# Filler transposes of a delta-rule kernel: on a PSUM tile that nobody reads, or left out

## The chip, the cores and the metric

The kernel runs on one core of a Trainium2 chip. The metric is the device time of one execution in microseconds (us); the lower, the better. Engines: PE (TensorE), DVE (VectorE), ACT (ScalarE), POOL (GpSimd) and SP, which issues the DMAs.

## The reference

Three stages follow each other, in fp32. First a delta-rule recurrence over 768 positions for 4 batches of 8 heads, each with a 48 x 48 state:

```
k_n = k / (norm(k) + 1e-06)
for t in range(768):
    y[t]  = q[t] @ state
    v_old = state^T k_n[t]
    state = state + beta[t] * outer(k_n[t], v[t] - v_old)
```

Then a gated MLP with mixing over positions:

```
h = relu(x @ w_in)                      # 384 -> 1024
u, v = h[..., :512], h[..., 512:]
v_n = layer_norm(v)
v_s = w_spatial @ v_n + b_spatial       # over the 768 positions
x = (u * v_s) @ w_out                   # 512 -> 384
```

Then a rotation with a second mixing over positions:

```
theta = x @ w_theta
y = w_tok_r @ (x * cos(theta)) + w_tok_i @ (x * sin(theta))
u = x + y
out = u + relu(u @ w_ch)
```

## The kernel before

The recurrence is worked in 48 chunks of 64 positions, 12 for each batch, one after the other; all 8 heads of a batch go together. I call a chunk a step, numbered 0 to 47. Eight steps make a round, and for each round the inverse of 32 small triangular matrices is needed ahead of its first step. The large matrix products of the later stages (L1050; three fp32r products for each fp32 one) have no part in the recurrence, and those whose batch is through with it are set between its steps.

What a step does, with the lines of the profile:

- `chain`: L906 (PE, into PSUM `ru`), L910 (DVE subtracts, giving `rt`), L920 (PE, into `ru`), two copies of `ru` into the state tile `W` (ACT or DVE, L482 or L488), L936/L938 (PE, into PSUM `s`), two copies of `s` into the next `W`. Each needs the one before it. L948/L949 (PE, into `py`) give the output.
- `gram`, for a step eight to twelve later: L711/L716 (PE, into PSUM `gp`), read by DVE at L736 (`GX`) and L740 (`pp`). A mask from POOL (L671) goes in.
- `jit`: L845/L846 (PE, into PSUM `m`), rounds 0 and 1 only.
- `invert`, once for each round: some 60 dependent DVE instructions (L779, L791) and three transpositions (L757, L795, L800), then twice L818 (PE, into `gp`), ACT copies `gp` to `ct`, L824 (PE, into `gp`), ACT copies `gp` to `GX`. L920 of the round's first step needs the result.

`gp` is one PSUM tile of two banks, `GPt`, used by L705, L711, L716, L818 and L824. `ru` is another, `RUt`, of which L906 and L920 use columns 0 to 95 of each bank.

The order of the instructions on every engine is made by a list scheduler, `Plan.run`, at build time. It holds a model of durations and of the clock of PE, which is granted at one of two levels. Where its model has PE idle for a while ahead of a task, and the activity of PE is low, it puts `k` constant transposes of the identity matrix ahead of the task (`self.filler(k)`, L514). They compute nothing that is used; they keep the array busy. They write columns 0 to 127 of `GPt`. The scheduler doesn't model what `gp` is doing at that time, but the program waits for it: a write to `gp` follows the last reads of it, and a read of `gp` that comes later in the program follows that write. A large product is chosen in place of a small task (`pe_pick`) when the modelled activity of PE, fillers included, is low. In the first inversion there is a burst of fillers besides (`BURST0`, 60 of them).

Of the kernel before, what the change touches and what calls it, by code (L numbers as in the profile page):

```python
# [97 lines left out]
BANK = 180.0  # L98
# [34 lines left out]
class Half(Buf):  # L133
# [6 lines left out]
    t = property(lambda self: self.whole.t[:, self.i], lambda self, x: None)  # L140
# [10 lines left out]
def P0_READY(plan, free):  # L151
    t = plan.ident
    return t.end is not None and t.end + t.extra + 1000.0 < free


class Plan:
# [76 lines left out]
    def pe_pick(self, l, s0, c):  # L233
# [27 lines left out]
            return best  # L261
        return c

    def run(self):
        self.warm, self.win, self.acc, self.burst = False, 0, 0.0, False
        self.hist = []
# [19 lines left out]
        free = dict.fromkeys(self.ENGS, 0.0)  # L286
        held = dict.fromkeys(self.ENGS, 0)
        lock = {"DVE": (0.0, 0.0), "POOL": (0.0, 0.0)}
        mode = 0
        lands, dmaq = [0.0] * LANES, 0.0  # L290
        cand = [t for t in self.tasks if t.left == 0]
        n = 0
        while cand:
            per = {}
            for t in cand:
# [9 lines left out]
                for e, dur in t.opts:  # L305
                    r = 0.0
                    for d in deps:
                        x = d.end + d.extra + (self.SAME[e] if d.eng == e else self.TAIL[d.eng] + self.LAT[e])
                        if x > r:
                            r = x  # L310
                    for b in t.banks:
                        o = b.last
                        if o is not None and o.eng != e and o.end + BANK > r:
                            r = o.end + BANK
# [9 lines left out]
                    k = s + dur + (0.0 if t.crit else BIAS[e])  # L324
# [16 lines left out]
            s, e, t, dur = pick  # L341
            t.eng, t.start, t.end = e, s, s + dur
            if e == "PE":
                gap = s - free[e]
                if s < FILL_END and self.warm and not t.big and P0_READY(self, free[e]):
                    need = 0
                    for win in (SLIDE, FILL_WIN):
                        h = s + dur - win
                        a = dur * t.act
                        for x0, x1, ac in reversed(self.hist):  # L350
                            if x1 <= h:
                                break
                            a += (x1 - max(x0, h)) * ac
                        need = max(need, int((FILL_LOW * win - a) // 78.0) + 1)
                    room = int((gap - FILL_EDGE) // 82.0)
                    more = max(need, int(FILL_ACT * gap // 82.0))
                    k = max(min(need, FILL_K), min(room, more))
                    if k > 0:
                        f0 = free[e] + (100.0 if mode else 0.0)
                        f1 = self.pe_run(PEFILL, f0, 82.0 * k)[0]  # L360
                        self.hist.append((f0, f1, PEFILL.act))
                        mode = 0
                        self.filler(k)
                        self.filled += k
                        s = max(s, f1)
                        t.start, t.end = s, s + dur
                if t.mode != mode:
                    t.start = s = s + (100.0 if mode else 140.0)
                mode = t.mode
                t.end = self.pe_run(t, s, dur)[0]  # L370
                self.hist.append((s, t.end, t.act))
                if t.big:
                    self.credit -= dur
# [26 lines left out]
class Bytes(float):  # L400
    n = 0
# [40 lines left out]
def kernel(  # L442
# [18 lines left out]
    nc = tc.nc  # L461
    mm = nc.tensor.matmul
    eng = {"ACT": nc.scalar, "DVE": nc.vector, "POOL": nc.gpsimd, "SP": nc.sync}
    P = Plan()
# [13 lines left out]
    def ring(pl, tag, shape, dtype=F32, bufs=1):  # L478
        return Ring(pools, pl, shape, dtype, tag, bufs)
# [28 lines left out]
        return [("SP", x)]  # L508


    def filler(n):

        for _ in range(n):
            nc.tensor.transpose(GPt[:, 0:128], ident.t, ident.t)  # L514

    P.filler = filler

# [17 lines left out]
    def single(pl, name, shape, dtype=F32):  # L535
        return Buf(tile_=pools[pl].tile(shape, dtype, name=name))

    ident = single("const", "ident", [128, 128])
# [10 lines left out]
    GPt = pools["ps_a"].tile([128, 1024], F32, name="gp")  # L549
    r_gp = Fixed(pools, "ps_a", GPt, "gp")  # L550
    RUt = pools["ps_a"].tile([128, 2, 512], F32, name="ru")
    r_ru = Fixed(pools, "ps_a", RUt[:, :, 0:2 * D], "ru")
    r_s = ring("ps_a", "s", [128, HP, D], F32, 1)
    PYt = pools["ps_a"].tile([128, HP, 128], F32, name="py")
    PY = Buf(tile_=PYt)
# [40 lines left out]
    def rnd(g):  # L596
        return divmod(g, RM)
# [590 lines left out]
    for g in range(NG):  # L1188
        r, j = rnd(g)
# [341 lines left out]
```

## Time and profile before

| | us |
|---|---|
| median of 3 runs | 807.89 (805.58 to 807.99) |
| the profiled execution | 812.74 |
| its span, first to last instruction | 811.0 |
| PE busy | 740.4 |
| DVE busy | 569.6 |
| ACT busy | 400.2 |
| L514 (filler), PE busy, 352 instructions | 63.3 |

The page gives the busy time of each engine, the chain of work that ended last, and groups of instructions by line. The trace behind it answers by line, by stage and in order of time. A busy PE is not PE at its peak: the rows of matmuls include the time that a result takes to come out, and at the lower clock they are longer. Idle time in front of an instruction is put down to what came last; a reader should look which engine then waited for which, and in which stage, since shares over the whole span mix stages with different limits.

### The profile page before, as it was taken

Reading aid. Unit: us, or ns where it says so; the run is one execution under the profiler, and the core shown is the slowest. Engines: PE = TensorE matmul, PEld = TensorE weight load, DVE = VectorE, ACT = ScalarE, POOL = GpSimd, SP = SyncE. Lnnn points to the kernel's source line nnn. Section 1 sums busy time; section 2 is a strip of 40 time slices with the busy share of each in tenths; the row PEclk is TensorE's granted clock in tenths of the full one; section 3 lists DMA queues with packets and bytes.
Section 4 is the critical chain, followed back from the end, with each engine's and each line's share of the span. In section 5 each row is a group of like instructions: output and inputs, shape, how many; then the busy total and the mean of one; then the engine's idle time right before and its main releaser. Section 6 shows DMA issues by size and latency. Waiting matters only on the chain.

```text
span 811.0 us, 22761 instructions
## 1 busy us (share of the span) xinstructions
PE 740.4 (91%) x9281; PEld 681.0 (84%) x9281; DVE 569.6 (70%) x1398; ACT 400.2 (49%) x878; POOL 154.4 (19%) x169
## 2 busy tenths in 40 slices
PE   4486889889887988998999999999999999999998
PEld 4385667768776776787898999999999999999997
DVE  5988797997991696994458745679565575556545
ACT  4837357657542455885567636155333342333321
POOL 2035344351421202141001100012111111111100
PEclk9999789989996699998999999999999999999999
DMA  7617567875776376776887720153020011002001
GB/s 217 205 44 205 153 178 196 242 207 153 208 217 195 108 213 204 217 220 178 244 261 244 220 90 1 65 161 109 25 84 27 27 37 53 25 26 83 1 1 59
DMA packets 93272, 109.56 MB, mean 135 GB/s; under 512 B 10096, under 2 KB 73968, under 8 KB 93168
## 3 DMA queue, kind: packets, MB, share of 16 engines
q1 hardware_dynamic: 93168, 108.11, 45.0%
q8 instruction: 73, 1.20, 0.6%
q14 instruction: 31, 0.25, 0.1%
HBM read 79.76 MB, written 26.61 MB: 131 GB/s over the span
## 4 chain that ended last, share of the span: by engine, by line
PE 64%; DVE 17%; DMA 6%; ACT 5%; issue 5%; SPq 2%; POOL 1%; POOLq 0%; DVEq 0%; ACTq 0%
PE m L1050 30%; PE y L1050 19%; PE gp L514 6%; DVE un L791 4%; DVE tmp L779 4%; DMA k<-in_vkn_dram 2%; DMA xr<-xd 2%; PE gp L824 1%; PE py L948 1%; DVE GX L736 1%; PE gp L818 1%; ACT ct L482 1%; PE s L936 1%; PE ru L920 1%; PE m L1357 1%
## 5 line engine op out<-in xcount | busy, mean ns | idle before, releaser
L1050 PE MATMUL m<-w,vh 128*128 128x256 f32 x576 | 112.1, 294 | 0.4 <-ACT uT L482 0.4
L1050 PEld LDWEIGHTS m<-w,vh 128*128 128x128 f32 x576 | 90.8, 194 | 3.3 <-ACT uT L482 0.6
L1050 PE MATMUL y<-wr,xTh 128*128 128x384 f32 x432 | 86.2, 337 | 0.0
L514 PE MATMUL gp<-ident 128*128 128x128 f32 x352 | 63.3, 327 | 24.3 <-DVE pp L740 8.1
L1050 PE MATMUL y<-w,xTl 128*128 128x384 f32 x432 | 83.9, 336 | 0.0
L1050 PE MATMUL m<-w,vl 128*128 128x256 f32 x288 | 82.1, 285 | 0.0
L1050 PEld LDWEIGHTS y<-wr,xTh 128*128 128x128 f32 x432 | 75.3, 188 | 0.0
L1050 PEld LDWEIGHTS y<-w,xTl 128*128 128x128 f32 x432 | 75.1, 188 | 0.0
L514 PEld LDWEIGHTS gp<-ident 128*128 128x128 f32 x352 | 47.9, 166 | 30.5 <-DVE pp L740 10.0
L791 DVE TENSOR_TENSOR un<-un,tmp 128x30 f32<-128x30 f32 (+21 forms) x209 | 71.0, 350 | 1.5
L779 DVE TENSOR_TENSOR tmp<-un 128x30 f32<-128x30 f32 (+21 forms) x209 | 67.6, 333 | 1.5
L1050 PEld LDWEIGHTS m<-w,vl 128*128 128x128 f32 x288 | 55.8, 194 | 0.0
L671 POOL TENSOR_TENSOR gm<-mask,ng 128x384 f32<-128x384 f32 (+1 forms) x52 | 43.2, 836 | 56.3 <-DVE pp L740 26.3
L1382 DVE TENSOR_SCALAR bgr<-m 128x384 int32<-128x384 f32 x22 | 12.2, 555 | 55.3 <-PE m L1050 55.3
L482 ACT ACTIVATE W<-ru 64x192 f32<-64x192 f32 x87 | 28.4, 326 | 45.9 <-PE ru L920 43.4
L1050 PE MATMUL m<-wo,gh 128*128 128x384 f32 x176 | 44.7, 334 | 0.0
L1050 PE MATMUL m<-xTh,wih 128*128 128x256 f32 x144 | 43.6, 303 | 0.9 <-ACT hv L482 0.9
L1050 PE MATMUL m<-xTl,wih 128*128 128x256 f32 x144 | 40.8, 283 | 0.0
L1050 PE MATMUL m<-xTh,wil 128*128 128x256 f32 x144 | 40.7, 283 | 0.0
L482 ACT ACTIVATE x<-m 128x384 f32<-128x384 f32 x13 | 6.4, 491 | 65.7 <-PE m L1050 65.7
L482 ACT ACTIVATE W<-s 48x192 f32<-48x192 f32 x78 | 25.6, 328 | 26.2 <-PE s L938 25.0
L1050 PE MATMUL m<-uh,wc 128*128 128x384 f32 x144 | 38.5, 337 | 0.0
(213 smaller groups left out, 1933.1 us busy)
## 6 DMA issues: line engine op xcount, KB each, us to landing
kq<-in_kqT_dram SPq DMA_DIRECT2D x96, 128.0 KB, 3.5
vk<-in_vkn_dram SPq DMA_DIRECT2D x48, 192.0 KB, 3.7
kg<-in_kgT_dram SPq DMA_DIRECT2D x32, 256.0 KB, 3.4
gd<-gt SPq DMA_DIRECT2D x24, 256.0 KB, 3.8
graw<-gd SPq DMA_DIRECT2D x24, 256.0 KB, 3.1
k<-in_vkn_dram SPq DMA_DIRECT2D x24, 192.0 KB, 4.0
xd<-xs SPq DMA_DIRECT2D x48, 96.0 KB, 3.0
xr<-xd SPq DMA_DIRECT2D x24, 192.0 KB, 3.2
```

The source lines that it names most:

```text
L482: nc.scalar.activation(out=out, in_=in_, func=func, **kw)
L514: nc.tensor.transpose(GPt[:, 0:128], ident.t, ident.t)
L671: eng[e].tensor_tensor(out=gm.t[:, lo:hi], in0=mask.t.unsqueeze(1).to_broadcast([128, hi - lo, CH]), in1=ng_b[r].t[:, j, 4 + lo:4 + hi].un ...
L736: A(o_dve(256), lambda e: nc.vector.tensor_tensor(out=gxj, in0=GX0()[:, :, 0] if fused else pv(), in1=gm.t[:, 2:6], op=ALU.mult), [ps, gm] ...
L779: eng[e].tensor_tensor(out=t3, in0=un.t[:, k:k + 1, 0:k].to_broadcast([128, m, k]), in1=un.t[:, t0:32:st, k:k + 1].to_broadcast([128, m, k ...
L791: eng[e].tensor_tensor(out=un.t[:, t0:32:st, 0:k], in0=un.t[:, t0:32:st, 0:k], in1=t3, op=ALU.add)
L818: mm(out=pv[q + 32:q + 64, u, :], lhsT=gx[q:q + 32, u0 + u, 32:64], rhs=un.t[q:q + 32, u0 + u, :], start=True, stop=True, tile_position=(q ...
L824: mm(out=pv[q:q + 32, u, :], lhsT=ct.t[q + 32:q + 64, u, :], rhs=gx[q + 32:q + 64, u0 + u, 32:64], start=True, stop=True, tile_position=(q ...
L920: mm(out=pu.t[o:o + 64, h, q * D:(q + 1) * D], lhsT=gx[i:i + 64, j * HP + slot(hp), :], rhs=rt.t[i:i + 64, hp, :], start=True, stop=True)
L936: mm(out=pss.t[0:48, hp, :], lhsT=kt[64:128, hp, :], rhs=w[64:128, 0, hp, :], start=f, stop=l, skip_group_check=True)
L1050: mm(out=view(), lhsT=a, rhs=c, start=(start and q == 0 and s_ == 0), stop=(stop and q == tot - 1 and s_ == 2))
L1382: P.add(o_dve(DM), lambda e: nc.vector.tensor_scalar(out=ni.t.bitcast(I32), in0=th(), scalar1=1.0 / TWO_PI, scalar2=None, op0=ALU.mult), [ ...
```

## The change

The filler gets an argument for where it writes. `P.spots` lists two buffers, `gp` and `ru`. Before the scheduler puts fillers ahead of a task, `spot` looks for the first of the two whose last issued user has, in the plan, been written and read to the end a margin (`BANK`, 180 ns) before the fillers would start. Fillers go there: to `GPt[:, 0:128]`, or to columns 128 to 255 of the first bank of `RUt`. If both are in use, there are no fillers at that place. The burst of the first inversion stays on `gp`.

```diff
+    def spot(self, f0):
+
+        for r in self.spots:
+            b = r.issued[-1] if r.issued else None
+            if b is None or all(t.end is not None and t.end + BANK <= f0 for t in (*b.writers, *b.readers)):
+                return r.tag
+        return None
...
-                    if k > 0:
-                        f0 = free[e] + (100.0 if mode else 0.0)
+                    f0 = free[e] + (100.0 if mode else 0.0)
+                    spot = self.spot(f0)
+                    if k > 0 and spot is not None:
                         f1 = self.pe_run(PEFILL, f0, 82.0 * k)[0]
                         self.hist.append((f0, f1, PEFILL.act))
                         mode = 0
-                        self.filler(k)
+                        self.filler(k, spot)
...
-    def filler(n):
-
+    def filler(n, spot="gp"):
+        out = GPt[:, 0:128] if spot == "gp" else RUt[:, 0, 128:256]
         for _ in range(n):
-            nc.tensor.transpose(GPt[:, 0:128], ident.t, ident.t)
+            nc.tensor.transpose(out, ident.t, ident.t)
...
+    P.spots = [r_gp, r_ru]
```

The scheduler's model sees other activity of PE afterwards, and so the whole order changes. Of 352 fillers 172 are left, 104 on `gp` (73 of them in one row at the start) and 68 on `ru`, in 20 rows of the order where there were 60. Lines behind the added method are 8 to 10 higher: L514 becomes L523, L818 L828, L824 L834, L920 L930, L1050 L1060.

Two places of PE's order show it. The first is the inversion of round 3, between steps 23 and 24. Before:

```order
L514 MATMUL gp<-ident 128x128 x5
L818 MATMUL gp<-un,GX_110 32x32 x32
L514 MATMUL gp<-ident 128x128 x13
L824 MATMUL gp<-GX_110,ct 32x32 x32
L514 MATMUL gp<-ident 128x128 x13
L818 MATMUL gp<-un,GX_110 32x32 x32
L514 MATMUL gp<-ident 128x128
L920 MATMUL ru<-rt,GX_110 64x48 x8
L514 MATMUL gp<-ident 128x128 x8
L824 MATMUL gp<-GX_110,ct 32x32 x32
```

And of the changed kernel, from the last pair of output matmuls of step 23 on:

```order
L959 MATMUL py<-kq,W_109 48x64
L523 MATMUL ru<-ident 128x128 x6
L834 MATMUL gp<-GX_110,ct 32x32 x32
L523 MATMUL ru<-ident 128x128 x13
L828 MATMUL gp<-un,GX_110 32x32 x32
L523 MATMUL ru<-ident 128x128
L930 MATMUL ru<-rt,GX_110 64x48 x8
L834 MATMUL gp<-GX_110,ct 32x32 x32
L523 MATMUL ru<-ident 128x128 x8
```

The fillers between the halves of the inversion write `ru` now; those ahead of the first half are gone, two and the output matmuls having moved behind it.

The second place is step 30, from its L906 on, ahead of the inversion of round 4. Before:

```order
L949 MATMUL py<-kq,W_109 48x64
L906 MATMUL ru<-W_108,kq 64x48 x8
L514 MATMUL gp<-ident 128x128 x3
L920 MATMUL ru<-rt,GX_110 64x48 x8
L514 MATMUL gp<-ident 128x128 x6
L936 MATMUL s<-W_108,vk 48x48
```

Of the changed kernel, the same step (`m` is the PSUM of the large products, `xTh`/`xTl` and `wih`/`wil` the two parts of x and of w_in):

```order
L916 MATMUL ru<-W_108,kq 64x48 x8
L1060 MATMUL m<-xTh,wih_140 128x256
L1060 MATMUL m<-xTl,wih_140 128x256
L1060 MATMUL m<-xTh,wil_143 128x256
L1060 MATMUL m<-xTh,wih_141 128x256
L1060 MATMUL m<-xTl,wih_141 128x256
L1060 MATMUL m<-xTh,wil_144 128x256
L930 MATMUL ru<-rt,GX_110 64x48 x8
```

Where fillers stood between L906 and L920, six large products of batch 1 stand now. Up to the last L920 the order has 126 products of 128x512 and 672 of 128x256, where there were 108 and 594. On DVE 382 rows stand ahead of the `rt` (L910) of step 8, where there were 333; ahead of that of step 23 it is 618 and 613.

## Rows read from the trace of the kernel before

**Rows 1.** The page: its line of the chain by line, and L514's group.

```profile
PE m L1050 30%; PE y L1050 19%; PE gp L514 6%; DVE un L791 4%; DVE tmp L779 4%; DMA k<-in_vkn_dram 2%; DMA xr<-xd 2%; PE gp L824 1%; PE py L948 1%; DVE GX L736 1%; PE gp L818 1%; ACT ct L482 1%; PE s L936 1%; PE ru L920 1%; PE m L1357 1%
...
L514 PE MATMUL gp<-ident 128*128 128x128 f32 x352 | 63.3, 327 | 24.3 <-DVE pp L740 8.1
```

**Rows 2.** By stage: stretch and length, engines' busy us, PE clock, DMA share, GB/s.

```profile
41.00:61.60 20.60, 18.56 (x329) 17.09 (x327) 16.52 (x48) 7.69 (x14) 7.52 (x8) 1.00 0.18 51
61.60:134.60 73.00, 58.98 (x1289) 48.66 (x1288) 61.15 (x165) 41.71 (x99) 31.11 (x38) 0.88 0.66 182
134.60:242.10 107.50, 95.85 (x2061) 81.33 (x2058) 98.71 (x268) 61.38 (x141) 38.98 (x44) 0.95 0.72 205
242.10:274.30 32.20, 26.46 (x441) 22.57 (x441) 9.62 (x24) 10.29 (x18) 4.76 (x5) 0.61 0.53 154
274.30:320.80 46.50, 40.65 (x824) 33.65 (x823) 38.55 (x89) 25.03 (x47) 11.10 (x10) 0.94 0.64 189
320.80:410.70 89.90, 87.48 (x1567) 73.90 (x1566) 62.53 (x170) 62.86 (x137) 13.83 (x14) 0.96 0.76 220
410.70:811.00 400.30, 395.11 (x2499) 387.60 (x2498) 250.23 (x503) 164.21 (x336) 41.75 (x37) 1.00 0.24 78
```

**Rows 3.** The same for L514 alone: PE, PE weight load, clock, DMA.

```profile
61.60:134.60 73.00, 20.82 (x105) 14.83 (x104) 0.88 0.66 182
134.60:242.10 107.50, 4.67 (x24) 2.76 (x24) 0.95 0.72 205
242.10:274.30 32.20, 14.79 (x65) 11.47 (x65) 0.61 0.53 154
274.30:320.80 46.50, 8.87 (x56) 5.88 (x55) 0.94 0.64 189
```

**Rows 4.** View of line L514, who waited for it: us, times.

```profile
  ACT ct L482: 9.4, 5
...
  DVE pp L740: 6.5, 5
```

**Rows 5.** Timeline of step 3: start us, us, engine, instruction [idle before, its releaser].

```profile
88.29 0.34 DVE L910 TENSOR_TENSOR rt<-ru,vk 128x192 f32<-128x192 f32 x1
...
88.42 3.15 PE L514 MATMUL gp<-ident 128*128 128x128 f32 x14 [1.71 <-DVE pp L740]
...
91.50 0.65 PE L920 MATMUL ru<-rt,GX 64*64 64x48 f32 x16
```

**Rows 6.** Timeline of the inversion of round 3, steps 23 and 24.

```profile
244.68 2.64 PE L514 MATMUL gp<-ident 128*128 128x128 f32 x15 [2.17 <-DVE GX L736]
...
247.35 0.43 DVE L740 TENSOR_TENSOR pp<-gp,gm 128x256 f32<-128x256 f32 x1 [2.23 <-PE gp L514]
...
249.30 1.20 PE L818 MATMUL gp<-un,GX 32*32 32x32 f32 x64
...
251.79 2.48 PE L514 MATMUL gp<-ident 128*128 128x128 f32 x13 [1.29 <-ACT ct L482]
...
254.21 1.92 PE L824 MATMUL gp<-GX,ct 32*32 32x32 f32 x64
...
257.41 3.04 PE L514 MATMUL gp<-ident 128*128 128x128 f32 x13 [1.29 <-ACT GX L482]
...
262.63 0.68 PE L920 MATMUL ru<-rt,GX 64*64 64x48 f32 x16
...
264.04 1.97 PE L514 MATMUL gp<-ident 128*128 128x128 f32 x8 [0.73 <-ACT ct L482]
```

**Rows 7.** Timeline behind step 47, large products, PE.

```profile
418.45 0.40 PE L1050 MATMUL m<-wih,xTh 128*128 128x512 f32 x1
418.69 0.40 PE L1050 MATMUL m<-wil,xTh 128*128 128x512 f32 x1
...
424.00 0.28 PE L1050 MATMUL m<-xTh,wih 128*128 128x256 f32 x1
424.12 0.28 PE L1050 MATMUL m<-xTl,wih 128*128 128x256 f32 x1
```

## The prediction

> **What bounds the kernel now.** I read the page first. TensorE (PE) is busy for most of the span; L514, the constant transposes of the filler, is 352 instructions in 63.3 us, with 24.3 us of idle time just before them, of which VectorE (DVE) reading `gp` ended the largest piece; and the chain that ended last lies on that line for 6% of the span, about 50 us [rows 1]. A filler computes nothing, so this is what the change touches. Then the table by stage, cut at the first L920 of steps 0, 8, 23, 25, 32 and 47 of the recurrence [rows 2]. It shows three regimes. From 410.7 us PE is busy for all but some 5 us of 400: the end is simply the recurrence's end plus the large products (L1050) still left. From 320.8 to 410.7 PE is at 97% (87.48 of 89.90 us). Before that PE has holes: subtracting busy time from length in the four rows from 61.6 to 320.8 leaves 14.0, 11.7, 5.7 and 5.9 us idle, 37 us, and the filler takes 20.82, 4.67, 14.79 and 8.87 us [rows 3]. So between 61.6 and 320.8 us PE spends about 86 us on nothing useful. DVE is the second bound there: 98.71 of 107.50 us in 134.6:242.1, 61.15 of 73 before it, but only 9.62 of 32.20 in 242.1:274.3, where everybody waits for everybody.
>
> Why the filler costs time is in the view of its line and in the timeline. It writes `gp`. Each of its instructions therefore waits until the last readers of `gp` are through, and the readers that come later wait for it: ACT `ct` 9.4 us, DVE `pp` 6.5 us [rows 4]. At 88.42 fourteen of them have waited 1.71 us for `pp` and run 3.15 us, while `rt`, which the next real step needs, is made by 88.63; L920 starts at 91.50 [rows 5]. In the inversion of round 3 it is worse: L818, ScalarE's copy, filler, L824, copy, filler, L818 follow each other with no overlap [rows 6].
>
> **The change part by part.** The compiled order has 172 fillers where there were 352: the 73 at the start stay, 68 others go to `ru`, 31 stay on `gp` at places where its last reader is planned to be done, 180 are gone. The scheduler plans anew with that, so the order of everything moves.
>
> *Start, 41 to 61.6 us.* Behind the burst of 73 stand 31 fillers in and around the first inversion. They now run beside the copies. The eight at 264.04 take 1.97 us at half clock [rows 6], so one is about 0.12 us at full clock; 31 of them and 2.04 us of idle PE [rows 2] are 5.8 us at most, and the copies themselves stay. I take 3.
>
> *Steps 0 to 8, 73.0 us.* 20.82 us of filling go almost entirely (104 to 11 instructions up to L920 of step 8). But the freed time isn't all gain: counting DVE's rows ahead of the `rt` of step 8, 382 stand there now and 333 before. Those 49, each by the duration of its twin in the trace, are some 16 us of DVE work pulled forward, of which about 5 ran before the end of the stage already. 61.15 + 11 = 72 us of DVE work don't fit in less than 73 to 76 us. I give this stage a loss of 3, which cancels the start.
>
> *Steps 8 to 23, 107.5 us.* What was pulled forward is missing here: ahead of the `rt` of step 23 only 5 DVE rows more stand than before, so the stage has some 9 us less on DVE (98.71 to 89.7). At the present 92 to 94% that is 96 us: 11 us gained. PE allows it: 95.85 less 4.67 of filler and 4.2 of products that moved ahead of the stage is 87 us.
>
> *Steps 23 to 25, 32.2 us.* Here the clearest gain lies [rows 6]. L818 starts at 249.30, behind 15 fillers (2.64 us) that waited for `GX` and for which `pp` then waits 2.23 us. Without them `pp` runs 2.2 us earlier and L818 can follow at about 245.7: 3.6 us. From L818 to L920 of step 24 the trace has 13.33 us. In the new order 8 fillers and a `py` group (taken as six fillers more) stand beside the first copy and 13 fillers beside the second, on `ru`, so that the longer of the two counts and not the sum: 1.2 + 1.65 + 1.2 + 1.55 + 1.2 = 6.8 us at full clock (L818's 1.20 at 249.30), about 10.6 at half clock (L824's 1.92 at 254.21). Gain 2.7 to 6.5. In step 24 the eight at 264.04 wait for `ct` ahead of L824; behind it and on `ru` they cost 0.3 to 1.8 us less, and the small fillers up to step 25 are gone, 1.5. Sum 8 to 13.4; as nobody waits for a filler any more, the clock should stand nearer to full, but the row of this stage says 0.61 now, so I take the middle, 10.5.
>
> *Steps 25 to 32, 46.5 us.* This stage takes up work. 18 products of 128x512 and 78 of 128x256 are ahead of the last L920 that weren't before (126 and 672, against 108 and 594), and here is where most join: with the filler gone the planner sees an idle array and gives it a product. PE was 40.65 us, less 8.87 filler, plus 13.5: 45.3 of 46.5 us. It will be the bound; I allow 3 us more length.
>
> *Steps 32 to 47.* 23 fillers now stand here (about 2.8 us), 1 us of products is gone, and PE has 2.4 us to spare: 0.
>
> *After step 47.* The 18 + 78 products no longer stand here. By starts that follow each other one is 0.24 us or 0.12 us [rows 7] (0.232 and 0.119 over longer runs), so 4.2 + 9.3 = 13.5 us, straight off the end, as PE is 99% busy. The first product that needs a new weight stands about as far behind step 47 as before, so nothing new should be late; I allow 1.5 us.
>
> Sum: -3 + 3 - 11 - 10.5 + 3 - 13.5 + 1.5 = -30.5 us. Against this stands what the rows can't price: PE without filler sits idle more often, and its clock may fall. It was granted 0.88 in steps 0 to 8 and 0.61 in 242.1:274.3 even with fillers [rows 2], since they stood waiting themselves. From below, no more cold time than now costs 0 (or gives a little back in 242.1:274.3); from above, if steps 0 to 8 run wholly at 1.2 GHz, the lower of the two levels, some 36 us of real PE work there become about 60, still under DVE's 72, and cost a few tenths per hand-over, some 5 us, and as much again in steps 8 to 23. Mostly hidden by DVE, it is nearer to the lower end; I take 4.5. That leaves **-26 us**. The profiled execution took 812.74 us for a span of 811.0, so its successor should be near 787; the median of the runs, 807.89, lies 4.85 lower, and I forecast **782 us**.
>
> The Trainium skill, page "TensorE: Matmul & The Clock Gate", part "The HAM clock gate", speaks against the change: the array's default state is the throttled one, and only activity releases it. By that rule 180 transposes fewer cost clock wherever nothing replaces them, which is the first rival; this trace bears it out only in part, as the stage with the lowest clock, 0.61, is also the one with the most filler per us.
>
> **The rivals.**
>
> *The clock decides, and it gets slower.* Place: steps 0 to 23, where almost no filler is left and products are few. The bare PE work there is about 36 + 84 = 120 us at 2.4 GHz, up to 85% longer at 1.2 (L824: 1.92 against 1.20; products double). The two stages last 180.5 us, and elsewhere the change still gives some 22 (inversion and products at their lower ends). With PE 95% full at most, 126 x (1 + 0.85c) = 202.5 gives c = 0.71: if PE is at the lower level for more than 71% of these stages the whole is slower; at 85% it would be 217 us there and 14 more than now in all: 822. For it: 0.88 and 0.95 are granted with fillers, some of which will have helped. Against: those are cold shares of 24 and 10%, and would have to become four times as large; the 0.95 was reached with 24 fillers in 107.5 us.
>
> *The moved products don't pay.* If steps 25 to 32 become wholly PE-bound and the recurrence waits for each product, the stage grows by what it took in, 13.5 instead of 3, and inputs of these products that land later than planned take 4 more: -11.5, 796. For it: PE would be 97% full. Against: 320.8 to 410.7 runs 97% full with just this mix.
>
> *The recurrence isn't bound by PE.* If steps 0 to 23 are held by DVE and loads alone and gain nothing, the inversion (10.5) and the products (13.5) less 8 of clock and stalls remain: -16, 792. For it: DVE at 92%, the DMA engines at 0.72 there.
>
> *The wait only moves to `ru`.* Eleven groups write `ru`, and L906 and L920 write it too; where ScalarE is later than planned, a filler waits for its copy and holds up PE as in rows 5, at 1.7 us each [rows 5]. If all do: 19 us of the gain gone, 801. Against: the groups of round 0 stand before the first use of `ru`, the others at least an L818 or L824 behind the last L920.
>
> *The change doesn't do what it says:* the scheduler's times are a plan, and where the chip is later, the fillers on `gp` still wait. But of 279 beyond the burst only 31 are left there, so for 808 the re-planned order would have to lose elsewhere all that is won, and I see no row for that.
>
> **How the numbers follow.** Forecast -26 with a spread of 8 either way: 0.55. Recurrence not bound by PE 0.13, products that don't pay 0.12, `ru` 0.08, nothing 0.03, clock 0.09, of which 0.01 ends within 0.3%. A measurement of this kernel can tell about 0.3% (2.4 us) from no change. Faster 0.55 + 0.13 + 0.12 + 0.08 = 0.88; same 0.04; slower 0.08. The range reaches from 765, where clock, stalls and the lengthening of steps 25 to 32 cost nothing (9), the inversion runs at full clock (3) and steps 8 to 23 are as full as DVE allows (5), to 801, the dearest of the smaller rivals; the clock case and the tails stay outside, under 2 in 10.
>
> **What would show it.** Right: the filler's line with under 15 us busy beyond the burst and hardly an idle time ended by DVE `pp`; L818 to L920 of step 24 in 7 to 10 us, not 13.3; step 23 near 231, step 25 near 253, step 47 near 397 us; then 388 us to the end. Wrong: a granted clock under 0.7 in steps 0 to 23; steps 25 to 32 over 53 us; PE waiting for a load or a copy in the 40 us behind step 47. The forecast falls if step 47 is reached at 405 or later, as then only the products are left.

## The result and the profile after

The changed kernel takes **786.50 us** (median; 785.66 to 791.06) where the kernel before took 807.94 beside it: a ratio of 0.9736, with a 95% interval of 0.9673 to 0.9799. Forecast were 782 us and a range of 765 to 801. The profiled execution of the changed kernel took 785.66 us, its span is 783.9 (before: 812.74 and 811.0).

The changed kernel by stage, cut as in [rows 2] at the first L930 (before: L920) of steps 0, 8, 23, 25, 32 and 47. The columns are the stretch and its length, the busy us of PE, PE's weight load, DVE, ACT and POOL, then PE's clock, the DMA share and GB/s:

```profile
41.00:59.80 18.80, 18.80 (x327) 17.54 (x326) 15.66 (x43) 6.83 (x11) 7.55 (x7) 1.00 0.20 56
59.80:136.70 76.90, 61.67 (x1283) 52.34 (x1286) 71.94 (x203) 50.42 (x121) 36.06 (x42) 0.68 0.68 195
136.70:237.90 101.20, 91.61 (x1983) 78.62 (x1975) 90.72 (x236) 50.67 (x112) 39.91 (x47) 0.91 0.72 205
237.90:253.10 15.20, 12.78 (x407) 10.83 (x406) 8.53 (x23) 9.50 (x18) 1.35 (x2) 1.00 0.84 252
253.10:304.80 51.70, 48.30 (x900) 40.70 (x900) 46.82 (x115) 34.07 (x73) 11.10 (x11) 0.97 0.71 214
304.80:398.10 93.30, 88.06 (x1533) 74.86 (x1528) 63.69 (x158) 61.15 (x125) 13.77 (x15) 0.96 0.75 224
398.10:783.90 385.80, 381.52 (x2403) 374.47 (x2402) 243.61 (x489) 157.07 (x323) 40.09 (x36) 1.00 0.23 74
```

Against [rows 2] the lengths changed by -1.8, +3.9, -6.3, -17.0, +5.2, +3.4 and -14.5 us; that is the whole of the 27.1 us between the spans. The execution before was 4.85 us above the median of its kernel's first three; by the medians the gain is 21.4 us. Two stages win clearly: the inversion of round 3 (32.2 to 15.2 us, and the clock there from 0.61 to 1.00) and the end behind step 47. Step 47 itself is reached only 12.6 us earlier (398.10 against 410.70).

The same stages for the filler alone, L523 (columns: PE, weight load, clock, DMA share, GB/s):

```profile
41.00:59.80 18.80, 14.54 (x102) 13.17 (x100) 1.00 0.20 56
59.80:136.70 76.90, 2.33 (x12) 1.63 (x11) 0.68 0.68 195
136.70:237.90 101.20, 1.02 (x4) 0.49 (x4) 0.91 0.72 205
237.90:253.10 15.20, 4.37 (x30) 3.23 (x30) 1.00 0.84 252
253.10:304.80 51.70, 0.00 (x0) 0.00 (x0) 0.97 0.71 214
304.80:398.10 93.30, 3.61 (x23) 2.47 (x23) 0.96 0.75 224
```

Behind the start the filler is 11.3 us where [rows 3] has 49.2. In the view of its line the two lists that follow, who made it wait and who waited for it, are empty; before, the first summed to 52.1 us, and the second, of which [rows 4] has two lines, to 26.2:

```profile
L523 PE MATMUL gp<-ident x104: 272/273/473, 40.2 to 340.7; 128*128 128x128 f32 x104
...
L523 PE MATMUL ru<-ident x68: 272/273/421, 52.2 to 249.8; 128*128 128x128 f32 x68
its engine sat idle before it (us, times) until:
who waited for it (us, times):
```

The inversion of round 3 in the changed kernel's timeline, which answers to [rows 6]:

```profile
238.50 1.20 PE L828 MATMUL gp<-un,GX 32*32 32x32 f32 x64 [0.19 <-DVE pp L750]
...
240.59 0.87 PE L523 MATMUL ru<-ident 128*128 128x128 f32 x6
241.39 1.07 PE L834 MATMUL gp<-GX,ct 32*32 32x32 f32 x56
...
243.21 1.64 PE L523 MATMUL ru<-ident 128*128 128x128 f32 x13
244.78 1.20 PE L828 MATMUL gp<-un,GX 32*32 32x32 f32 x64
...
246.17 0.45 PE L930 MATMUL ru<-rt,GX 64*64 64x48 f32 x16
```

From L828 to L930 are 7.67 us; the same way took 13.33 us in [rows 6]. The 13 fillers take 1.64 us, at full clock, and start while ScalarE copies `gp` to `GX`; before they took 3.04 us and started behind that copy, after 1.29 us of idle time.

### The profile page after: what moved, and what is told of

Same layout as the page of the kernel before. It is cut to its first block, busy times and chain, and to the rows that moved or that the text cites. A ratio compares the mean times of both kernels' runs of the same rounds, so it can differ in the third digit from the quotient of the medians.

```text
span 783.9 us, 22417 instructions
## 1 busy us (share of the span) xinstructions
PE 720.9 (92%) x9101; PEld 666.4 (85%) x9101; DVE 574.0 (73%) x1402; ACT 397.3 (51%) x871; POOL 155.2 (20%) x172
## 4 chain that ended last, share of the span: by engine, by line
PE 64%; DVE 17%; DMA 6%; ACT 6%; issue 4%; SPq 3%; POOL 1%; POOLq 0%; DVEq 0%; ACTq 0%
PE m L1060 32%; PE y L1060 20%; DVE tmp L789 4%; DVE un L801 3%; DMA bgr<-in_w_r_dram 2%; DMA vk<-in_vkn_dram 2%; PE gp L523 2%; ACT bgr L491 1%; SPq L528 1%; PE py L958 1%; PE gp L834 1%; PE ru L930 1%; PE m L1367 1%; PE gp L828 1%; PE ru L916 1%
## 5 line engine op out<-in xcount | busy, mean ns | idle before, releaser
L1060 PE MATMUL m<-w,vh 128*128 128x256 f32 x576 | 112.0, 294 | 0.7 <-DVE gt L1176 0.7
L1060 PEld LDWEIGHTS m<-w,vh 128*128 128x128 f32 x576 | 90.5, 193 | 3.6 <-DVE gt L1176 0.8
L1060 PE MATMUL y<-wr,xTh 128*128 128x384 f32 x432 | 86.2, 337 | 0.0
L1060 PE MATMUL y<-w,xTl 128*128 128x384 f32 x432 | 83.9, 336 | 0.0
L1060 PE MATMUL m<-w,vl 128*128 128x256 f32 x288 | 82.0, 285 | 0.0
L1060 PEld LDWEIGHTS y<-wr,xTh 128*128 128x128 f32 x432 | 75.3, 188 | 0.0
L1060 PEld LDWEIGHTS y<-w,xTl 128*128 128x128 f32 x432 | 75.1, 188 | 0.0
L801 DVE TENSOR_TENSOR un<-un,tmp 128x30 f32<-128x30 f32 (+21 forms) x209 | 73.6, 363 | 1.5
L789 DVE TENSOR_TENSOR tmp<-un 128x30 f32<-128x30 f32 (+21 forms) x209 | 70.0, 345 | 1.8
L1060 PEld LDWEIGHTS m<-w,vl 128*128 128x128 f32 x288 | 55.8, 194 | 0.0
L491 ACT ACTIVATE W<-ru 64x192 f32<-64x192 f32 x80 | 26.2, 327 | 53.8 <-PE ru L930 49.3
L681 POOL TENSOR_TENSOR gm<-mask,ng 128x384 f32<-128x384 f32 (+1 forms) x52 | 42.5, 822 | 39.5 <-DVE pp L750 14.1
L1060 PE MATMUL m<-xTh,wih 128*128 128x256 f32 x144 | 45.5, 316 | 0.1
L1060 PE MATMUL m<-wo,gh 128*128 128x384 f32 x176 | 44.7, 334 | 0.0
L1060 PE MATMUL m<-xTl,wih 128*128 128x256 f32 x144 | 42.2, 293 | 0.0
L1060 PE MATMUL m<-xTh,wil 128*128 128x256 f32 x144 | 42.1, 292 | 0.0
L1060 PE MATMUL m<-uh,wc 128*128 128x384 f32 x144 | 38.5, 337 | 0.0
L1406 DVE TENSOR_TENSOR bgr<-x,bgr 128x384 f32<-128x384 f32 x48 | 30.3, 646 | 9.9 <-ACT bgr L491 9.9
L491 ACT ACTIVATE bgr<-bgr 128x384 uint8<-128x384 uint8 x34 | 36.3, 1077 | 0.5
```

The costliest lines, as they stand in the source:

```text
L491: nc.scalar.activation(out=out, in_=in_, func=func, **kw)
L681: eng[e].tensor_tensor(out=gm.t[:, lo:hi], in0=mask.t.unsqueeze(1).to_broadcast([128, hi - lo, CH]), in1=ng_b[r].t[:, j, 4 + lo:4 + hi].un ...
L789: eng[e].tensor_tensor(out=t3, in0=un.t[:, k:k + 1, 0:k].to_broadcast([128, m, k]), in1=un.t[:, t0:32:st, k:k + 1].to_broadcast([128, m, k ...
L801: eng[e].tensor_tensor(out=un.t[:, t0:32:st, 0:k], in0=un.t[:, t0:32:st, 0:k], in1=t3, op=ALU.add)
L1060: mm(out=view(), lhsT=a, rhs=c, start=(start and q == 0 and s_ == 0), stop=(stop and q == tot - 1 and s_ == 2))
L1406: P.add(o_tts(DM), lambda e, src=src: eng[e].tensor_tensor(out=src.t, in0=x2.t, in1=src.t, op=ALU.mult), [x2], [src], pr)
```

## The experiments

Three causes are mixed in the result: the fillers' waits are gone, the clock of PE has changed, and the planner, seeing fewer fillers, wrote another order with more large products ahead of step 47. The experiments take them apart. Line numbers are those of the changed kernel; every ratio is against the kernel before, run beside it.

### The order of before, fillers moved or left out

The first kernel plans as if every filler were there, so its order is that of before; 107 fillers go to `ru` where `spot` finds it free, the other 245 to `gp`.

```diff
-                    if k > 0 and spot is not None:
+                    if k > 0:
...
-                        self.filler(k, spot)
+                        self.filler(k, spot or "gp")
```

> The order of before, all 352 fillers kept; 107 of them go to ru because the plan has it free, 245 stay on gp, and nothing is left out. Products move by nothing. Theory (false waits and moved products both count): the inversion of round 3 gets its overlap but most fillers on gp still wait, so 5 to 10 us faster than before, 798 to 803. Rival (the gain comes from the new order alone): within 3 us of 808.

Measured: 801.62 us, ratio 0.9927 (0.9887 to 0.9967). The second keeps that order too, but doesn't write the 103 fillers for which no tile is free:

```diff
-                    if k > 0 and spot is not None:
+                    if k > 0:
...
-                        self.filler(k, spot)
+                        self.filler(k if spot else 0, spot)
```

> The order of before; the 103 fillers for which the plan has no free tile are planned but not emitted, 107 go to ru, 142 stay on gp. Every other instruction stands where it stood before. Theory: the recurrence gets the waits back, step 25 some 15 us sooner, nothing from products, so 792 to 800. Rival 1 (products alone): 805 to 809. Rival 2 (fewer fillers cost clock and that is not hidden): 808 or more.

Measured: 794.24 us, ratio 0.9848 (0.9767 to 0.9930). Both came out as expected. In the view of the filler's line, the first kernel's list of who waited for it has shrunk to 8.0 us but is there; in the second it is empty:

```profile
who waited for it (us, times):
  DVE pp L750: 4.9, 4
  DVE GX L746: 1.9, 2
  PEld m L855: 0.7, 1
  ACT ct L491: 0.5, 1
```

The last stages of the first kernel, then of the second (from the inversion of round 3 on: steps 23 to 25, 25 to 32, 32 to 47, the rest):

```profile
236.30:257.70 21.40, 18.09 (x441) 15.66 (x441) 9.67 (x24) 9.17 (x17) 3.91 (x4) 0.92 0.67 200
257.70:306.20 48.50, 40.80 (x822) 33.67 (x821) 39.12 (x89) 26.19 (x49) 11.65 (x11) 0.95 0.67 196
306.20:401.20 95.00, 90.94 (x1567) 76.62 (x1566) 63.13 (x170) 63.16 (x137) 13.89 (x14) 0.92 0.70 211
401.20:802.00 400.80, 395.36 (x2499) 387.50 (x2498) 249.67 (x503) 163.83 (x336) 41.77 (x37) 1.00 0.24 77
```

```profile
233.90:255.30 21.40, 17.85 (x413) 15.46 (x414) 9.97 (x24) 9.56 (x17) 4.60 (x5) 0.66 0.74 218
255.30:304.80 49.50, 46.17 (x816) 38.35 (x816) 39.05 (x90) 24.92 (x47) 10.98 (x10) 0.78 0.63 185
304.80:392.50 87.70, 85.42 (x1567) 71.83 (x1566) 63.40 (x170) 62.59 (x137) 13.60 (x14) 0.99 0.76 228
392.50:792.40 399.90, 394.92 (x2499) 387.46 (x2498) 249.72 (x503) 164.06 (x336) 41.74 (x37) 1.00 0.24 77
```

The number of PE instructions behind step 47 is that of [rows 2] (2499), and so is the time there, 400.8 and 399.9 against 400.3: no product has moved. All that these kernels gain lies in the recurrence, which reaches step 47 at 401.2 and 392.5 where it was 410.7. So with no change of order at all, moving the fillers is worth about 9 us and leaving the rest out another 9. The changed kernel reaches step 47 later than the second one, at 398.1, but has 385.8 us left instead of 399.9. By the spans the steps are 811.0, 802.0, 792.4 and 783.9: **about a third each for the destination, for what is left out, and for the new order.** These are single executions, and two of the same kernel differ by up to 3.3 us here (783.9 and 787.2 for the changed kernel), so the thirds are rough.

Read by place, they look different. Step 25 is reached at 274.3 us before, at 257.7 in the first kernel, 255.3 in the second and 253.1 in the changed one. Up to there 16.6 us come with the destination alone, 2.4 with leaving out and 2.2 with the new order. Of its 16.6 us the first kernel loses 7.1 again in steps 25 to 47, 5.1 of them in steps 32 to 47, where neither it nor the kernel before has a filler. More than half of that is the clock: the beginning of that stage took 9.0 us at 0.52, and 5.4 us at 1.00 in the kernel before, PE without a pause in both (the first kernel's row, then that of before):

```profile
306.20:315.20 9.00, 9.00 (x138) 7.03 (x137) 4.60 (x18) 4.97 (x11) 0.00 (x0) 0.52 0.68 203
```

```profile
320.80:326.20 5.40, 5.40 (x138) 4.20 (x137) 3.70 (x15) 3.88 (x11) 0.00 (x0) 1.00 0.87 269
```

What the second kernel gains over the first, 9.6 us, lies for 7.3 us in the same steps 32 to 47 (95.0 and 87.7 us, at 0.92 and 0.99 of the clock). All four times of the second (792.86 to 797.02) are under all ten of the first (798.87 to 805.52), so the difference is real; that it comes from leaving out waits and fillers at the places where they stood is not shown.

### The order of after, all fillers back on `gp`

The opposite: exactly the changed kernel's order and its 172 fillers, with the 68 on `ru` written to `gp` again.

```diff
-                        self.filler(k, spot)
+                        self.filler(k, "gp")
```

> The order of the changed kernel to the last instruction; only the 68 fillers on ru are written to gp again. Theory (the wait of and for gp costs where fillers stand inside an inversion): steps 23 to 25 longer by 3 to 8 us than the changed kernel's 15.2, and the first inversion (to L920 of step 0) by 1 to 2; 790 to 797 in all. Rival (only what is left out counts, the tile does not): 784 to 789, with 23 to 25 under 17 us.

Measured: 791.17 us, ratio 0.9769 (0.9694 to 0.9844), as expected; L930 of step 0 comes 1.3 us later (61.1 against 59.8), as expected too. Its steps 23 to 25, and two rows of its timeline there:

```profile
237.50:258.20 20.70, 16.46 (x406) 14.02 (x406) 8.56 (x23) 9.47 (x18) 1.37 (x2) 0.75 0.59 185
```

```profile
244.29 2.47 PE L523 MATMUL gp<-ident 128*128 128x128 f32 x13 [1.29 <-ACT GX L491]
...
246.69 1.92 PE L828 MATMUL gp<-un,GX 32*32 32x32 f32 x64
```

The wait for ScalarE's copy is back with the very 1.29 us of [rows 6], and the stage takes 20.7 us instead of 15.2. Here the second effect is seen too: PE, standing in that wait, was granted the lower clock soon after (0.75 in the stage; the 13 fillers 2.47 us against 1.64, L828 1.92 against 1.20). A filler that waits doesn't keep the array busy. As wholes, the intervals of this kernel and the changed one overlap; of the stage there are two profiles of the changed kernel, with 15.2 and 15.4 us, and this one with 20.7.

### Is the clock in steps 0 to 8 the price?

Those steps ran at 0.88 before and run at 0.68 now. Since there are two levels, 0.68 means half clock for 2 x 0.32 x 76.9 = 49 us, against 2 x 0.12 x 73.0 = 18 us. Two kernels change the rule at step 8: one plans with the old rule (all fillers; on `gp` where the plan has nothing free, but on `ru` where only that is free) until L930 of step 8 is planned and with the new one behind it; the other the reverse.

```diff
-                    if k > 0 and spot is not None:
+                    if k > 0 and (spot is not None or self.mark.end is None):
...
-                        self.filler(k, spot)
+                        self.filler(k, spot or "gp")
...
+        P.mark = marks[8]
```

(The reverse has `is not None` in the last place.)

> The old rule until L920 of step 8 is planned, the new one behind it: steps 0 to 8 keep their fillers, 244 fillers in all, and 8.5 us of products instead of 13.5 stand earlier than before. Theory (steps 0 to 8 are bound by DVE, the clock at 1.2 GHz for 44 us there costs next to nothing): 787 to 795, no better than the changed kernel. Rival (the long stretch at the lower clock costs, fillers would have kept it up): under 784, with steps 0 to 23 at least 5 us shorter than in the changed kernel.

> The new rule until L920 of step 8 is planned, the old one behind it: 251 fillers, 4.3 us of products earlier than before. Theory: the inversion of round 3 waits as before, the products stay late, only steps 0 to 23 gain, so 797 to 804. Rival (the change pays in steps 0 to 8): under 795.

Measured: 796.63 us, ratio 0.9884 (0.9800 to 0.9968), for the old rule early, which is slower than expected; 795.88, ratio 0.9872 (0.9796 to 0.9947), for the old rule late, which is faster than expected. The two are equal, so the totals don't say which part of the kernel gained. The stages say more. With the old rule early, steps 0 to 23 take 179.2 us (71.2 and 108.0), 178.1 in the changed kernel, so its rival fell. It loses 6.9 us in steps 23 to 25, where it has no filler, and 9.3 behind step 47 (395.1 against 385.8); its steps 23 to 25:

```profile
238.30:260.40 22.10, 16.45 (x398) 14.91 (x398) 13.74 (x34) 13.63 (x23) 2.25 (x3) 0.54 0.85 255
```

With the old rule late, steps 23 to 25 take 18.1 us at 1.00 of the clock, not the 32.2 of before that I had expected: its old rule puts the fillers of that inversion on `ru` too, and L828 to L930 of step 24 take 6.79 us.

The stages also say something on the clock. Up to step 8 the late kernel and the one with fillers back on `gp` have the order of the changed kernel. Their rows for that stage, the late one first:

```profile
58.80:134.70 75.90, 58.80 (x1283) 50.45 (x1286) 71.89 (x203) 50.17 (x120) 35.80 (x41) 0.75 0.69 198
```

```profile
61.10:138.10 77.00, 64.56 (x1287) 54.18 (x1289) 68.30 (x201) 49.86 (x120) 35.94 (x41) 0.65 0.68 193
```

At 0.75, 0.68 and 0.65 of the clock the same order takes 75.9, 76.9 and 77.0 us: 16 us more at half clock cost 1 us, hardly more than the 0.7 us by which two executions of the changed kernel differ here (76.9 and 76.2, both at 0.68). The changed kernel's own stretches show why:

```profile
69.80:114.20 44.40, 36.07 (x594) 30.39 (x595) 44.12 (x113) 24.53 (x59) 24.57 (x28) 0.50 0.74 212
```

For 44.4 us on end PE is at half clock, and DVE is busy for 44.12 of them. The end of this stage is set by DVE, and a PE of half the speed still fits beside it.

### No fillers at all, and fillers on `gp` alone

One kernel writes no fillers but the 60 of the burst (`if k > 0 and spot is not None:` becomes `if False:`), the other lists one buffer only:

```diff
-    P.spots = [r_gp, r_ru]
+    P.spots = [r_gp]
```

> No fillers but the 60 of the burst; the order is planned anew with that, 11.3 us of products earlier than before. Theory (what fillers give in clock is hidden, what they cost is the waits): 783 to 792, like the changed kernel. Rival (the 112 fillers left keep the clock up where it counts): over 795, with more of steps 23 to 47 at 1.2 GHz than the changed kernel's 10.2 us.

> Fillers only where gp itself is free in the plan, never on ru: 97 instead of 172, 18.4 us of products earlier than before (13.5 in the changed kernel). Theory: 780 to 790, as the fillers on ru cost and give little; 5 us more of products come off behind step 47. Rival (the ru fillers are worth their place, in the inversions): over 792.

Measured: 796.64 us, ratio 0.9813 (0.9747 to 0.9879), and 794.06, ratio 0.9782 (0.9715 to 0.9848). Both missed: I expected them as good as the changed kernel, and the times are those of the rivals (over 795 and over 792). The rival's condition for the first came as well: steps 23 to 47 are at half clock for 39 us, 10 in the changed kernel. But those steps are only 2.3 us longer (162.5 against 160.2); what that kernel loses lies in steps 8 to 23, 113.7 us against 101.2, where its order gives DVE 98.56 us of work instead of 90.72 (this was the slowest of its four executions):

```profile
132.70:246.40 113.70, 97.05 (x2177) 82.87 (x2175) 98.56 (x260) 55.41 (x125) 37.84 (x45) 0.89 0.68 195
```

Steps 23 to 25, without fillers first:

```profile
246.40:264.50 18.10, 14.46 (x288) 12.98 (x284) 14.14 (x36) 10.49 (x18) 4.49 (x4) 0.67 0.73 229
```

```profile
233.70:261.60 27.90, 17.22 (x406) 15.87 (x406) 16.28 (x35) 12.43 (x22) 5.12 (x5) 0.63 0.70 208
```

Neither has a filler there. The second one's rows of PE and ScalarE show what 27.9 us against 15.2 consist of:

```profile
243.69 1.91 PE L828 MATMUL gp<-un,GX 32*32 32x32 f32 x64 [1.29 <-ACT GX L491]
...
250.88 1.92 PE L834 MATMUL gp<-GX,ct 32*32 32x32 f32 x64 [4.67 <-ACT ct L491]
```

```profile
247.99 0.54 ACT L491 ACTIVATE bgm<-bgr 128x384 f32<-128x384 f32 x1 [4.35 <-DMA bgr<-in_w_out_dram]
...
249.64 1.19 ACT L491 ACTIVATE ct<-gp 32x512 f32<-32x512 f32 x2
```

The four L828 and L834 run at half clock, 1.92 us instead of 1.20: 2.9 us. The last of them waits 4.67 us for `ct` (0.71 in the changed kernel), because ScalarE's order has a step of a weight's preparation ahead of that copy, and ScalarE stood 4.35 us for that weight's load: 4.0 us. And 30 large products (5.67 us) stand in the stage, where the changed kernel has 0.04 us of them. Together 12.6 of 12.7 us; smaller waits, and the 4.37 us of fillers that are gone, are not in this sum, so that it comes out so closely is partly chance. So the 30 fillers on `ru` (4.37 us, the clock at 1.00) are worth having here: they lie beside copies. But the larger part of this loss is the other order that the planner wrote, a load at an unlucky place in it among it, and that isn't the fillers' doing.

### Taking more products ahead

The planner takes a large product instead of a small task when PE's modelled activity is below a number of its own, `HAM_T`. With fillers gone this rule fires more often, and that moved the products. A higher number takes more:

```diff
-HAM_T = .42
+HAM_T = .6
```

> The changed kernel with one number of the scheduler raised (HAM_T 0.42 to 0.60), so that it sets more products between the steps: 44.8 us earlier than before up to step 47, instead of 13.5. Theory (products are a gain only where PE would have been idle; from step 25 on it is 93 to 97% full): what comes off behind step 47 (31 us more) comes on before it, 780 to 792, step 47 at 420 to 432 instead of 398.1. Rival (every product moved ahead is won): 755 to 765.

Measured: 783.39 us, ratio 0.9645 (0.9577 to 0.9712), as expected. Step 47 comes 31.4 us later than in the changed kernel and the time behind it is 31.6 us shorter, so the spans are as good as equal (783.7 and 783.9), and the 31 us of products that it takes ahead beyond those of the changed kernel won nothing; they came off at one place and on at the other:

```profile
429.50:783.70 354.20, 350.46 (x2175) 344.61 (x2174) 222.31 (x429) 138.76 (x285) 35.91 (x33) 1.00 0.21 69
```

To settle so small a difference the changed kernel, this one, and one with .8 were run side by side for longer.

> The changed kernel once more, beside the two that pull more products, on one chip. Both theories: 784 to 790, ratio 0.970 to 0.978.

> HAM_T 0.60 again, on the same chip as the changed kernel. Theory (products pulled ahead are a gain only into idle PE time): 1 to 6 us faster than the changed kernel, 780 to 786. Rival (the first comparison was between chips): within 1 us of it.

> HAM_T 0.80: 74.7 us of products earlier than before up to step 47 (13.5 in the changed kernel, 44.8 at 0.60), 243 fillers. Theory: PE was near full between the steps at 0.60 already, so step 47 moves out by what comes off behind it, 779 to 790; the recurrence ends at 450 or later. Rival (each product moved ahead is won): under 770.

Measured: the changed kernel 786.52 us, ratio 0.9747 (0.9694 to 0.9799); with .6 784.95, ratio 0.9718 (0.9665 to 0.9770); with .8 831.25, ratio 1.0314 (1.0249 to 1.0380). The result is confirmed. With .6 it is 1.6 us faster beside it, inside the overlap of the intervals: at least as good, perhaps a little better. With .8 I was plainly wrong. Its stages from step 8 on (steps 8 to 16, 16 to 23, 23 to 25, 25 to 32, 32 to 47, the rest):

```profile
136.30:221.20 84.90, 77.00 (x1319) 67.50 (x1312) 76.33 (x196) 30.76 (x69) 27.95 (x31) 0.83 0.47 137
221.20:283.60 62.40, 53.92 (x1044) 47.01 (x1047) 44.17 (x112) 37.20 (x71) 15.01 (x17) 0.78 0.77 229
283.60:297.40 13.80, 13.21 (x214) 11.16 (x206) 13.60 (x47) 7.05 (x17) 3.20 (x4) 0.98 0.71 207
297.40:379.70 82.30, 74.28 (x1088) 65.18 (x1087) 61.62 (x157) 51.86 (x95) 7.24 (x7) 0.88 0.74 224
379.70:500.10 120.40, 111.14 (x1678) 94.78 (x1678) 56.42 (x139) 61.17 (x139) 7.56 (x9) 0.97 0.50 145
500.10:829.60 329.50, 322.20 (x1965) 318.35 (x1965) 204.14 (x387) 122.05 (x250) 34.16 (x32) 0.99 0.19 61
```

Behind step 47 it has 56.3 us less than the changed kernel, but steps 0 to 47 take 440.8 us instead of 338.3, 102.5 more. Of these 53.4 are the products themselves (198.9 against 145.5 us of L1060 in those stages) and 15 more idle time of PE (the lengths less PE's busy time: 50.8 against 35.9). Fillers are 13.2 (24.6 against 11.3), since the planner puts more where the recurrence stands alone again, and the remaining 21 us, by subtraction, are the steps' own PE work; its instructions are as many as in the changed kernel and on average longer (L930 254 ns against 238, L834 204 against 192), with the clock at 0.83, 0.78 and 0.88 in three of the stages. A product taken ahead paid its own time back and no more; here its place cost 49 us on top. Why the clock fell in stages with so many products was not pursued.

## Why the prediction was right, point by point

- **False waits.** Right, and the main cause up to step 25: there 16.6 of 21.2 us come with the destination alone, in the order of before, and the reverse brings 1.29 us of wait at one copy and 5.5 us of a stage back on `gp`. Of the whole, moving and leaving out without a new order give two thirds (802.0 and 792.4 of 811.0 to 783.9); how much of the second third is waits, and how much the fillers' own time and the clock behind them, is not shown.
- **Start, -3:** measured -1.8.
- **Steps 0 to 8, +3:** +3.9. The reason holds too: DVE has 71.94 us of work there, 72 forecast, and is 99% busy over 44 us.
- **Steps 8 to 23, -11:** -6.3, the term that was too good. The work was right (DVE 90.72 us, forecast 89.7), the filling was not: 90% instead of the 93% that I carried over from [rows 2]. Of the 10.5 us in which DVE is idle, 1.4 lie in the first 11.6 us, which run at half clock, and 6.9 between 175 and 213 us, where the clock is 0.93 or more; the longest waits of DVE are for a load of x (3.2 us) and for POOL's mask (2.1 us). In the second profile of the changed kernel the stage took 104.9 us. I took for granted that a stage keeps its share of holes when work leaves it.
- **Steps 23 to 25, -10.5 (8 to 13.4):** -17.0, beyond the range. From L930 of step 23 to L828 it was 7.24 us and is 0.63: 6.6 won, 3.6 forecast. L828 to L930 of step 24 took 7.67 us (6.8 at full clock forecast, 10.6 at half): 5.7 won, 2.7 to 6.5 forecast. From there to step 25 it was 11.69 us and is 6.93: 4.8 won, 1.8 to 3.3 forecast. I left out that the new order moves work across the cut: DVE's last transposition of the inversion (1.99 us at 241.93 us before) now ends ahead of L930 of step 23. In the order of before the stage takes 21.4 us in both kernels, so 10.8 us are the fillers' and some 6 the order's. I also took the middle because the row before said 0.61. In the first kernel, with that order and all 65 fillers of the stage, but on `ru` where it is free, the clock was 0.92 and L828 to L930 took 6.79 us: a low clock that came with the waits was no basis for what comes without them. Waits are not all of it: with no filler there at all the clock was 0.54 to 0.67.
- **Steps 25 to 32, +3, and 32 to 47, 0:** +5.2 and +3.4. The second stage had 2.4 us of PE's time to spare, and its PE work grew by 0.6; yet PE is idle for 5.2 us of 93.30 now. It was no longer held by PE alone, and I had reckoned as if it were. The first took in 17.5 us of products (30.95 us of L1060 against 13.50 of L1050), not 13.5.
- **After step 47, -13.5 + 1.5:** -14.5. The products come off at their own length, and PE waits there once, 0.7 us.
- **Clock, +4.5:** not a row by itself. Half clock in steps 0 to 8 rose from 18 to 49 us, where the upper bound of the working had the whole stage; between kernels of one order 16 us of it cost about 1. The argument for it (DVE's 72 us cover PE at half clock) was right for that stage. It is no rule for the next: in steps 16 to 23 two executions of the changed kernel, with about 7 and 14 us at half clock, took 49.5 and 53.3 us; that the clock alone made this difference is not shown. The allowance has about the size of what steps 8 to 23 lack, which is no confirmation of it.
- **Sum:** -27.1 against -26, and that close by luck: steps 23 to 25 gave 6.5 us more than forecast and the end 2.5 more, the others 12.4 less, and 4.5 were allowed for the clock. The profiled execution was forecast at 787 and took 785.66. That the median came out at 786.5 and not at 782 is the step from the execution to the median: before, the profiled one lay 4.85 us above its median, after, 0.84 below it. By the medians the gain is 21.4 us where 26 were forecast.

Of the signs named ahead, these came: no wait of DVE `pp` for it, L828 to L930 in 7 to 10 us, step 25 near 253 (253.1), step 47 near 397 (398.1), then 388 (385.8). Filler beyond the burst is 15.7 us (26.7 in all, 10.95 of them the burst), just above the 15 named. Step 23 came at 237.9, not near 231. Of the signs against, a clock under 0.7 came for steps 0 to 8 (0.68), not for 8 to 23 (0.91); over both it is 0.81.

**The rivals.** That the clock decides fell: it would have needed half clock for more than 71% of steps 0 to 23; the two rows give (49.2 + 18.2) / 178.1 = 38%. (The stage at 0.61 has the most filler per us only among those of [rows 3]: the start has more, 14.08 us of 20.60, at 1.00.) That the wait moves to `ru` fell: nobody waited for a filler. That moved products don't pay fell for the 14.5 us moved here: the changed kernel reaches step 47 5.6 us later than the second kernel and has 14.1 us less behind it. It came true beyond them: 46 us (400.3 less 354.2) gave the span that 14.5 gave, and 71 (400.3 less 329.5) lost. That the recurrence isn't bound by PE is half right: steps 0 to 8 gained nothing, and the gain of steps 8 to 23 fell short.

**Open.** About a third of the gain depends on which order the planner happens to write. The four kernels with yet other orders (old rule early or late, no fillers, `gp` alone) took 794 to 797 us; for one a load at a bad place was found, and nothing that ranks all of them. Also open is why the clock in steps 32 to 47, without a filler, differs between the two kernels in the order of before.

## What to carry to other kernels

Work that is only there to keep an engine busy must be free of every dependence: look at what the instruction ahead of it and the reader behind it do with its target, not only at its duration, since here a third of the gain, and 16.6 us up to step 25, came from moving 107 fillers without leaving out one. Where an engine's clock is low in a stretch, first ask whether that engine ends the stretch; beside a DVE that is 99% busy, 16 us more at half clock cost about 1 us, but where PE itself never paused, the same work took 9.0 us instead of 5.4. And an independent product set ahead of the end of a chain is a gain only while the engine has holes there: 14 us gave some 8, the next 31 nothing that stands out from the noise, and 71 made the kernel 3% slower than it was at first.

## What the runs showed of the hardware

- PE was at half clock for 44.4 us on end while its rows show it busy for 36.07 of them (the row of 69.80 to 114.20 above).
- A wait and the clock go together: 13 transposes took 1.64 us where they stood beside a copy, and 2.47 us, in the same order, where they stood behind it; in the order of before the clock of the stage was 0.61 with the waits and 0.92 with most of them gone. It is not the wait alone: in the second kernel 13 transposes that had not waited took 3.03 us, PE being at half clock already.
- Two executions of one program needn't get the same clock: steps 16 to 23 of the changed kernel took 49.5 us in one and 53.3 in the other profile, with about 7 and 14 us of them at half clock.
- Where PE ran without a pause, half clock cost what the row says: 138 matmuls took 9.00 us at 0.52 and 5.40 us at 1.00.
